# Matmuls chained in program order from the first token block on, with finer steps between blocks and attention and a two-step weight preparation

## The chip, the core and the metric

The kernel runs on one core of a Trainium2 chip. The metric is the device time of one execution in microseconds (us); lower is better. The engines are TensorE (PE; PEld for its weight loads), VectorE (DVE), ScalarE (ACT), GpSimd (POOL) and SyncE (SP), which here only issues the DMAs. Each engine works through its own queue in the order in which the program was built; semaphores tie the queues together.

## What is computed

```python
# attention, q, k, v: (4, 8, 576, 64); rows see columns of their own and earlier blocks of 64
scores = q @ k.T / 8, masked
attn = softmax(scores)
x = (attn @ v) as (2304 tokens, 512)
# layer 1:  d_model 512, d_ff 1536
x = ((x @ w_a) * (x @ w_b)) @ w_out
# layer 2:
xn = x / sqrt(mean(x * x) + 1e-6) * rms_g
g = xn @ w_gate
out = (g * sigmoid(g) * (xn @ w_val)) @ w_out
```

All is float32. Matmuls take numbers of fewer bits, so most operands are split into a high and a low part, and one product becomes three matmuls (high by high, high by low, low by high).

## The kernel before

**Blocks.** The 2304 tokens are cut into five blocks (512, then four of 448 columns), which pass through layer 1 (b0 to b4) and then layer 2 (b5 to b9). In a block, `moe` runs over 12 slices of d_ff, `fc`. A slice takes 24 matmuls, called A here (L444 to L446, `mm<-xh,ab`). After every three slices follow 36 matmuls with the second weights, called O (L471 to L473, `mm<-hh,o`). A block thus has 288 A and 144 O. Between A and O stand the product `g` on DVE (L456) and its parts `hh` (ACT) and `hl` (POOL, or DVE for the last slice of three).

**Attention.** The 32 heads (8 per batch of 576 tokens) come from the generator `attention`. For head m it issues scores S (L289, L290: tile i of up to 128 rows has 128, 256, 384, 512 and, in two halves of 288, 576 columns), transposes T of head m-1 (L336, in groups of 4, 5, 5 and 1), and values V of head m-2 (L375). A score tile goes to DVE for its row maximum (L293, L295, L298), to ACT for the exponential (L301) and to POOL for the division by the row sum (L315). A transposed group is copied as `ph` by ACT (L353) and `pl` by DVE (L354). Scores have two PSUM banks, so tile i+2 waits until tile i has been read.

**How they are mixed.** Layer 1's block b0 needs batch 0, b1 the next, and so on. `main` and `att` are streams: after each step of `main` the loop lets `att` go on while it is behind a share (`PACE`) of the matmul time spent in `main`. If heads are missing when the last O of a block are near, `before_last` issues them all. It then calls `split_of`, which makes `xh` and `xl` of the next block; they have one buffer, so the block before must have read them.

**Weights.** `prepare` takes one of 72 pieces of weights through `decode` (ACT L131 and L132, DVE L133 and L134, POOL L135) and then `split` (high part ACT, low part DVE or POOL by turns). Layer 1's pieces are used at once and written to DRAM for later blocks; 9 are made before b0 and 27 in b0. Layer 2's 36 pieces are made in b1 to b4.

**What sets the order.** The framework's scheduler takes the instructions from the program and decides each engine's order at build time, by priority and by a model of when operands are ready. `behind` adds an order edge without a semaphore. Before the change no such edge concerns PE: the scheduler may move A, O, S, T and V past each other.

Of the kernel before, what the change touches and what calls it, by code (L numbers as in the profile page):

```python
# [16 lines left out]
P = 128  # L17
# [29 lines left out]
def tile_attention_moe_moe(  # L47
# [30 lines left out]
    wab = ctx.enter_context(tc.tile_pool(name="wab", bufs=3))  # L78
# [39 lines left out]

    def decode(st):
# [8 lines left out]
        dst = stage.tile([P, 4 * P], F32, tag="x", name="x", bufs=2)  # L128
# [18 lines left out]
    staged, prepared, wtiles = {}, [0], {}  # L147
# [9 lines left out]
    def prepare():  # L157

        i = prepared[0]
        if i >= len(w_pieces):  # L160
            return
        stage_loads(i + 3)
        layer, kind, f, y = w_pieces[i]
# [11 lines left out]
        x = decode(staged.pop(i))  # L175
        prepared[0] += 1
# [34 lines left out]
    def attention(pools, x_of, done):  # L211
# [62 lines left out]
        def score(m, i):  # L274
# [12 lines left out]
            for a, z in halves:  # L287
                ps = ps_s()
                pe.matmul(ps[:, 0:z - a], qh[:, o:nk], kk[:, a:z], start=True, stop=False)  # L289
                pe.matmul(ps[:, 0:z - a], ql[:, o:nk], kk[:, a:z], start=False, stop=True)  # L290
                pss.append(ps)
# [26 lines left out]
        def p_transposes(m):  # L318
            pt[m] = []
            at = [0, 0]  # L320
            for part, pieces in GROUPS:
# [12 lines left out]
                for o, j, i, perm in first + rest:  # L334
                    a = min(j * P, S - P)
                    pe.transpose(ps[:, o:o + P], pp[m, i][:, a:a + P], perm)  # L336
                    cost += P / 1.2
# [21 lines left out]
        def values(m):  # L359
# [5 lines left out]
            for a, e in ((0, R), (R, S)):  # L365
# [22 lines left out]
            del vv[m], pt[m]  # L388
            done[b] = done.get(b, 0) + 1
            return cost  # L390
# [6 lines left out]
        for m in range(NH + 2):  # L397
            if m >= 2:
                yield values(m - 2)
# [28 lines left out]
    def moe(layer, pools, xh, xl, n, ps_mm, acc, finish, before_fc, before_last):  # L428
        hp, tp = pools
        h = {}  # L430
        for t in range(NTH):
            fcs = range(t * TF, (t + 1) * TF)
            for fc in fcs:
# [5 lines left out]
                for wi in range(2):  # L439
                    ps = ps_mm()  # L440
                    wh, wl = w[:, 2 * wi, :], w[:, 2 * wi + 1, :]
                    for c in range(KC):
                        a, z = c * P, (c + 1) * P
                        pe.matmul(ps[:, 0:n], wh[:, a:z], xh[:, c, 0:n], start=(c == 0), stop=False)  # L444
                        pe.matmul(ps[:, 0:n], wh[:, a:z], xl[:, c, 0:n], start=False, stop=False)  # L445
                        pe.matmul(ps[:, 0:n], wl[:, a:z], xh[:, c, 0:n], start=False, stop=(c == KC - 1))  # L446
# [11 lines left out]
                    yield KC * mm3(n)  # L458
# [3 lines left out]
            for dm0 in range(0, KC, 2):  # L462

                banks = {dm: ps_mm() for dm in (dm0, dm0 + 1)}
                for ys in (range(TF - 1), range(TF - 1, TF)):
                    for dm, ps in banks.items():
                        for y in ys:
# [84 lines left out]
    n = 0  # L552
# [8 lines left out]
    def normed(t0, n):  # L561
# [15 lines left out]
        pe.matmul(ps[:, 0:n], rms["ones"], sh, start=True, stop=False)  # L577
        pe.matmul(ps[:, 0:n], rms["ones"], sl, start=False, stop=True)
# [15 lines left out]
    nxt = split_of(0, BLOCKS[0])  # L594
    for at, (layer, t0, n_tok) in enumerate(blocks):
# [14 lines left out]
        def before_fc(fc, at=at, layer=layer, following=following, norm=norm, got=got):  # L610
            if at == 0:
                if fc > 0:
                    for _ in range(TF):
                        if prepared[0] < len(w_pieces) // 2:
                            prepare()
            else:
# [4 lines left out]
                if layer == 0:  # L621
                    n = sum(BACKGROUND[:at]) + BACKGROUND[at] * (fc + 1) // FC
                    while prepared[0] < len(w_pieces) // 2 + n:
                        prepare()
# [95 lines left out]
```

## Time and profile before

| what | us |
|---|---|
| median of 3 runs (1185.93 to 1188.22) | 1187.19 |
| the profiled execution, its own time | 1193.02 |
| its span, first to last instruction | 1191.2 |
| PE busy in the span | 1132.8 |
| DVE, ACT, POOL busy | 710.1, 529.5, 489.1 |

The span is what the trace explains; times below are counted from its start. A busy PE is not PE at its full rate, because the records of matmuls overlap; how far apart matmuls start says more.

### The profile page before, as it was taken

The page shows a single profiled execution, that of the slowest core. Times are in us where ns is not written, and L with a number is a line of the kernel's source. Part 1 is how long each engine was busy: PE and PEld are TensorE (multiplying, and loading weights), DVE is VectorE, ACT ScalarE, POOL GpSimd, SP SyncE. Part 2 cuts the span into 40 slices and gives each one's busy share as a digit, 9 for nine tenths or more (in the row PEclk, how much of TensorE's full clock was granted, in tenths as well). Part 3 has the DMA queues.
Part 4 walks back from the last instruction along what each step waited for, and adds up shares of the span by engine and source line. Part 5 has one row for each costly group of instructions (what it writes and reads, how often), then busy time and mean ns, then how long its engine had stood idle before and what let it go on. Part 6 is the DMA issues. An engine that isn't in the chain of part 4 may idle for free.

```text
span 1191.2 us, 16081 instructions
## 1 busy us (share of the span) xinstructions
PE 1132.8 (95%) x5578; PEld 992.0 (83%) x5578; DVE 710.1 (60%) x1411; ACT 529.5 (44%) x1174; POOL 489.1 (41%) x474
## 2 busy tenths in 40 slices
PE   7888888989999889998999999999999999999998
PEld 5566667769989779898899998888999999999997
DVE  7869799997777787778945523323624534433222
ACT  7758776765655666556533312312312312211211
POOL 6748767776636565546535202112012112112110
PEclk9898988999999889999899999999999999999999
DMA  5436575879777667658898956655765765765760
GB/s 177 147 113 217 192 260 173 311 251 335 261 239 240 229 234 234 230 203 309 310 412 323 341 198 246 224 195 191 279 228 198 280 221 204 256 214 209 255 227 35
DMA packets 65905, 279.98 MB, mean 235 GB/s; under 512 B 12064, under 2 KB 22304, under 8 KB 45344
## 3 DMA queue, kind: packets, MB, share of 16 engines
q1 hardware_dynamic: 65824, 278.95, 66.3%
q8 instruction: 44, 0.72, 0.2%
q14 instruction: 37, 0.30, 0.1%
HBM read 231.74 MB, written 47.19 MB: 234 GB/s over the span
## 4 chain that ended last, share of the span: by engine, by line
PE 67%; DVE 9%; ACT 4%; DMA 3%; POOL 2%; issue 2%; DVEq 0%; POOLq 0%; ACTq 0%
PE mm L445 14%; PE mm L446 14%; PE mm L444 14%; PE mm L471 7%; PE mm L472 7%; PE mm L473 7%; PE t L336 2%; PE t L375 2%; POOL x L135 1%; DVE kk L254 1%; DVE x L133 1%; PE s L289 1%; DVE st L134 1%; PE s L290 1%; DVE pl L354 1%
## 5 line engine op out<-in xcount | busy, mean ns | idle before, releaser
L444 PE MATMUL mm<-xh,ab 128*128 128x448 f32 (+1 forms) x960 | 360.2, 377 | 6.1 <-DVE xf L387 2.1
L446 PE MATMUL mm<-xh,ab 128*128 128x448 f32 (+1 forms) x960 | 358.7, 374 | 0.3 <-POOL ab L107 0.2
L445 PE MATMUL mm<-xl,ab 128*128 128x448 f32 (+1 forms) x960 | 358.3, 373 | 0.0
L107 POOL TENSOR_TENSOR hl<-g,hh 128x448 fp32r<-128x448 f32 (+1 forms) x80 | 99.4, 1243 | 425.1 <-ACT hh L97 424.5
L444 PEld LDWEIGHTS mm<-xh,ab 128*128 128x128 f32 x960 | 181.5, 189 | 26.3 <-ACT ab L97 2.9
L446 PEld LDWEIGHTS mm<-xh,ab 128*128 128x128 f32 x960 | 181.6, 189 | 19.9 <-POOL ab L107 0.4
L445 PEld LDWEIGHTS mm<-xl,ab 128*128 128x128 f32 x960 | 181.9, 190 | 18.3
L471 PE MATMUL mm<-hh,o 128*128 128x448 f32 (+1 forms) x480 | 182.3, 381 | 5.0 <-ACT hh L97 3.5
L472 PE MATMUL mm<-hh,o 128*128 128x448 f32 (+1 forms) x480 | 179.4, 374 | 0.0
L473 PE MATMUL mm<-hl,o 128*128 128x448 f32 (+1 forms) x480 | 169.1, 374 | 0.9 <-POOL hl L107 0.9
L97 ACT ACTIVATE hh<-g 128x448 fp32r<-128x448 f32 (+1 forms) x120 | 70.5, 588 | 204.2 <-DVE g L456 203.7
L315 POOL TENSOR_SCALAR p<-p,st 128x128 f32<-128x128 f32 (+4 forms) x160 | 106.5, 677 | 106.4 <-DVE st L312 63.9
L456 DVE SCALAR_TENSOR_TENSOR g<-mm,asb 128x448 f32<-128x448 f32 (+1 forms) x120 | 76.1, 635 | 117.5 <-PE mm L446 116.6
L135 POOL TENSOR_TENSOR x<-x,st 128x512 uint32<-128x512 uint32 x72 | 104.9, 1461 | 70.3 <-DVE st L134 27.1
L453 DVE SCALAR_TENSOR_TENSOR asb<-mm,asb 128x448 f32<-128x448 f32 (+1 forms) x60 | 38.2, 636 | 144.7 <-ACT asb L452 144.7
L301 ACT ACTIVATE p<-s,st 128x128 f32<-128x128 f32 (+2 forms) x171 | 88.5, 520 | 69.3 <-DVE st L295 40.7
L481 DVE SCALAR_TENSOR_TENSOR acc<-mm,acc 128x448 f32<-128x448 f32 (+1 forms) x120 | 69.9, 627 | 70.6 <-PE mm L473 70.5
L471 PEld LDWEIGHTS mm<-hh,o 128*128 128x128 f32 x480 | 90.9, 190 | 18.2 <-ACT hh L97 5.3
L473 PEld LDWEIGHTS mm<-hl,o 128*128 128x128 f32 x480 | 90.3, 189 | 11.7 <-POOL hl L107 1.7
L452 ACT ACTIVATE asb<-mm 128x448 f32<-128x448 f32 (+1 forms) x60 | 33.4, 556 | 148.1 <-PE mm L446 148.1
L472 PEld LDWEIGHTS mm<-hh,o 128*128 128x128 f32 x480 | 91.3, 190 | 9.1
L336 PE MATMUL t<-ident,p 128*128 128x128 f32 x416 | 73.2, 295 | 3.1 <-POOL p L315 2.9
(99 smaller groups left out, 1645.2 us busy)
## 6 DMA issues: line engine op xcount, KB each, us to landing
ab<-wab SPq DMA_DIRECT2D x108, 1024.0 KB, 6.0
o<-wo SPq DMA_DIRECT2D x36, 1536.0 KB, 6.9
st<-in_w_ab_dram SPq DMA_DIRECT2D x48, 512.0 KB, 4.5
wab<-ab SPq DMA_DIRECT2D x12, 1024.0 KB, 4.5
st<-in_w_o_dram SPq DMA_DIRECT2D x24, 512.0 KB, 4.9
wab<-bg SPq DMA_DIRECT2D x24, 512.0 KB, 7.0
qr<-in_q_dram SPq DMA_DIRECT2D x64, 144.0 KB, 3.8
wo<-o SPq DMA_DIRECT2D x4, 1536.0 KB, 6.2
```

What stands on the lines that cost most here:

```text
L107: eng_lo.tensor_tensor(lo, src, hi.bitcast(F32), ALU.subtract)
L135: pool.tensor_tensor(x, x, lo, ALU.add)
L301: act.activation(pi[:, a:z], pss[x][:, 0:z - a], AF.Exp, bias=s[:, i:i + 1], scale=1.0, accum_out=s[:, 5 + i + x:6 + i + x],)
L315: pool.tensor_scalar(pi, pi, s[:, 5 + y:6 + y], 1.0, ALU.mult, ALU.mult)
L336: pe.transpose(ps[:, o:o + P], pp[m, i][:, a:a + P], perm)
L444: pe.matmul(ps[:, 0:n], wh[:, a:z], xh[:, c, 0:n], start=(c == 0), stop=False)
L445: pe.matmul(ps[:, 0:n], wh[:, a:z], xl[:, c, 0:n], start=False, stop=False)
L446: pe.matmul(ps[:, 0:n], wl[:, a:z], xh[:, c, 0:n], start=False, stop=(c == KC - 1))
L456: dve.scalar_tensor_tensor(g, ps[:, 0:n], UNSCALE, asb, ALU.mult, ALU.mult)
L471: pe.matmul(ps[:, 0:n], wh, hh, start=(y == 0), stop=False)
L472: pe.matmul(ps[:, 0:n], wl, hh, start=False, stop=False)
L473: pe.matmul(ps[:, 0:n], wh, hl, start=False, stop=(y == TF - 1))
```

## The change

Every matmul and transpose now goes through a helper that, once b0 begins, puts it behind the one that the program issued before it: the scheduler can no longer reorder PE. The generators yield after every three A or three O and after each half of the values, so that the program itself mixes them. `prepare` decodes one piece and splits the piece of the call before; `x` has three buffers and `wab` four. Pieces are paced by the time spent in the block instead of by slice.

```diff
-    wab = ctx.enter_context(tc.tile_pool(name="wab", bufs=3))
+    wab = ctx.enter_context(tc.tile_pool(name="wab", bufs=4))
...
+    def in_order(ins):
+        if fixed[0] and "pe" in gate:
+            behind(ins, "pe")
+        gate["pe"] = ins
+    def matmul(*args, **kw):
+        in_order(pe.matmul(*args, **kw))
+    def transpose(*args):
+        in_order(pe.transpose(*args))
...
-        dst = stage.tile([P, 4 * P], F32, tag="x", name="x", bufs=2)
+        dst = stage.tile([P, 4 * P], F32, tag="x", name="x", bufs=3)
...
     def prepare():
         i = prepared[0]
+        if decoded:
+            split_piece(*decoded.pop())
         if i >= len(w_pieces):
             return
         stage_loads(i + 3)
+        decoded.append((i, decode(staged.pop(i))))
+        prepared[0] += 1
+        if prepared[0] in (len(w_pieces) // 2, len(w_pieces)):
+            split_piece(*decoded.pop())
...
                 for y, (src, j, q0) in enumerate(seq):
-                    pe.matmul(
+                    matmul(
...
-            del vv[m], pt[m]
-            done[b] = done.get(b, 0) + 1
-            return cost
+                if a > 0:
+                    del vv[m], pt[m]
+                    done[b] = done.get(b, 0) + 1
+                yield cost
+                cost = 0.0
...
-                        pe.matmul(ps[:, 0:n], wl[:, a:z], xh[:, c, 0:n], start=False, stop=(c == KC - 1))
+                        matmul(ps[:, 0:n], wl[:, a:z], xh[:, c, 0:n], start=False, stop=(c == KC - 1))
+                        if c < KC - 1:
+                            yield mm3(n)
...
-                    if ys[-1] == TF - 1:
-                        continue
-                    yield 2 * (TF - 1) * mm3(n)
+                            if y < TF - 1:
+                                yield mm3(n)
...
     nxt = split_of(0, BLOCKS[0])
+    fixed[0] = True
...
+        total = (2 * FC * KC + FC * KC) * mm3(n_tok)
+        first = prepared[0]
+        more = (BACKGROUND[at] if at else len(w_pieces) // 2 - first) if layer == 0 else 0
         while main.step():
+            while prepared[0] - first < min(more, int(more * main.spent / total / 0.85 + 0.9)):
+                prepare()
```

In the changed program PE's instructions carry the helper's lines, L128 for matmuls and L131 for transposes; DVE's L313 to L374 are the L293 to L354 of before.

**The end of b1 on PE.** `mm<-hh,o` are the last O of b1, `mm<-xh,ab` the first A of b2, `vv` the values of the second last head that b2 needs. Before:

```order
L375 MATMUL t<-ph_4412,vv 128x64
L471 MATMUL mm<-hh,o 128x448
L472 MATMUL mm<-hh,o 128x448
L473 MATMUL mm<-hl,o 128x448
L471 MATMUL mm<-hh,o 128x448
L472 MATMUL mm<-hh,o 128x448
L473 MATMUL mm<-hl,o 128x448
L471 MATMUL mm<-hh,o 128x448
L472 MATMUL mm<-hh,o 128x448
L473 MATMUL mm<-hl,o 128x448
L444 MATMUL mm<-xh,ab 128x448
L445 MATMUL mm<-xl,ab 128x448
```

After, where the values are those of the last head that b2 needs:

```order
L128 MATMUL t<-ph_4648,vv 128x64
L128 MATMUL t<-pl_4649,vv 128x64
L128 MATMUL mm<-xh,ab 128x448
L128 MATMUL mm<-xl,ab 128x448
L128 MATMUL mm<-xh,ab 128x448 x2
L128 MATMUL mm<-xl,ab 128x448
L128 MATMUL mm<-xh,ab 128x448 x2
L128 MATMUL mm<-xl,ab 128x448
L128 MATMUL mm<-xh,ab 128x448
L128 MATMUL mm<-hh,o 128x448 x2
L128 MATMUL mm<-hl,o 128x448
```

Before, a score, transposes and the values of one more head stand among the first A of b2. Now all heads of b2 stand ahead of 9 A and all 36 last O of b1.

**A head's last transpose and its values on PE, in b1.** `t<-swap` at the head of the rows is the last transpose group of a head, the one of 64 columns. Before:

```order
L336 MATMUL t<-swap,p_3212 128x128
L289 MATMUL s<-kk,qh 128x384
L290 MATMUL s<-kk,ql 128x384
L473 MATMUL mm<-hl,o 128x448 x2
L289 MATMUL s<-kk,qh 128x512
L290 MATMUL s<-kk,ql 128x512
L473 MATMUL mm<-hl,o 128x448
L375 MATMUL t<-ph_3334,vv 128x64
L375 MATMUL t<-pl_3335,vv 128x64
L471 MATMUL mm<-hh,o 128x448
L472 MATMUL mm<-hh,o 128x448
L473 MATMUL mm<-hl,o 128x448
```

After:

```order
L131 MATMUL t<-swap,p_3415 128x128
L128 MATMUL t<-ph_3525,vv 128x64
L128 MATMUL t<-pl_3526,vv 128x64
L128 MATMUL mm<-xh,ab 128x448
L128 MATMUL mm<-xl,ab 128x448
L128 MATMUL mm<-xh,ab 128x448
L128 MATMUL t<-ph_3525,vv 128x512
L128 MATMUL t<-pl_3526,vv 128x512
L128 MATMUL t<-ph_3525,vv 128x448
L128 MATMUL t<-pl_3526,vv 128x448
L128 MATMUL t<-ph_3606,vv 128x320
L128 MATMUL t<-pl_3607,vv 128x320
```

Before, nine more matmuls of the block follow the rows shown, and then the ten values. Now only three A stand between; two values of 192 columns follow, and then the pair that needs the last transpose.

**DVE ahead of the copy `pl` of that last transpose, in b1.** Before:

```order
L293 MEMSET s 64x64
L295 TENSOR_REDUCE st<-s 128x1
L354 TENSOR_TENSOR pl_3177<-t,ph_3176 128x512
L293 MEMSET s 64x64
L134 SCALAR_TENSOR_TENSOR st<-st 128x512
L354 TENSOR_TENSOR pl_3177<-t,ph_3176 128x64
```

After:

```order
L318 TENSOR_REDUCE st<-s 128x1
L99 CAST qh<-qr 128x576
L318 TENSOR_REDUCE st<-s 128x1
L274 SCALAR_TENSOR_TENSOR kk<-kr,kk 64x576
L374 TENSOR_TENSOR pl_3186<-t,ph_3185 128x64
```

Now the two maxima of the 288-column scores and the key product `kk` of the next head stand ahead of the copy.

## Rows read from the trace of the kernel before

**Rows 1.** Windows: stretch, then busy us per engine; clock, DMA share, GB/s.

```profile
0.00:101.80 101.80, 81.47 (x367) 55.59 (x368) 79.59 (x227) 73.34 (x189) 66.36 (x79) 0.90 0.48 151
101.80:270.80 169.00, 151.27 (x707) 120.40 (x705) 153.66 (x301) 118.40 (x268) 128.70 (x114) 0.93 0.69 239
270.80:395.80 125.00, 124.14 (x699) 114.71 (x698) 93.38 (x228) 73.54 (x186) 72.66 (x81) 1.00 0.75 261
395.80:545.30 149.50, 139.99 (x753) 125.21 (x752) 113.22 (x266) 87.72 (x221) 85.55 (x97) 0.95 0.68 232
425.00:545.30 120.30, 118.50 (x662) 107.40 (x662) 92.70 (x212) 70.94 (x178) 68.25 (x76) 1.00 0.70 237
545.30:647.90 102.60, 97.01 (x460) 88.07 (x459) 67.73 (x92) 50.07 (x92) 49.26 (x39) 0.95 0.90 343
737.20:835.60 98.40, 98.40 (x436) 81.44 (x435) 33.38 (x49) 25.35 (x40) 14.66 (x11) 1.00 0.60 215
835.60:1186.40 350.80, 350.80 (x1732) 325.06 (x1731) 133.65 (x203) 77.51 (x137) 50.11 (x41) 1.00 0.61 218
```

**Rows 2.** Timeline of PE around the starts of b2 and b3.

```profile
405.18 0.33 PE L289 MATMUL s<-kk,qh 128*128 128x128 f32 x1 [2.65 <-ACT p L301]
...
418.58 1.07 PE L444 MATMUL mm<-xh,ab 128*128 128x448 f32 x3 [1.98 <-DVE xh L99]
...
421.67 0.69 PE L289 MATMUL s<-kk,qh 128*128 128x384 f32 x1 [1.17 <-ACT p L301]
...
557.57 0.47 PE L444 MATMUL mm<-xh,ab 128*128 128x448 f32 x1 [2.08 <-DVE xf L387]
```

**Rows 3.** Groups by line, PE, 270.8 to 395.8: counts of S, T, V.

```profile
L336 PE MATMUL t<-ident,p 128*128 128x128 f32 x89 | 14.4, 275 | 0.0
L290 PE MATMUL s<-kk,ql 128*128 128x288 f32 (+4 forms) x40 | 12.5, 313 | 0.0
...
L375 PE MATMUL t<-pl,vv 128*128 128x64 f32 (+4 forms) x41 | 11.9, 315 | 0.0
```

**Rows 4.** Groups by line, DVE, 101.8 to 270.8: last column the idle time before.

```profile
L107 DVE TENSOR_TENSOR o<-x,o 128x512 fp32r<-128x512 f32 x11 | 10.5, 957 | 1.2 <-ACT o L97 1.0
...
L107 DVE TENSOR_TENSOR ab<-x,ab 128x512 fp32r<-128x512 f32 x9 | 7.9, 880 | 2.6 <-ACT ab L97 2.6
```

**Rows 5.** Timeline of PE: transposes at 353, then values of one head.

```profile
352.74 0.82 PE L336 MATMUL t<-ident,p 128*128 128x128 f32 x6
353.40 0.27 PE L336 MATMUL t<-swap,p 128*128 128x128 f32 x1
...
301.45 0.39 PE L375 MATMUL t<-ph,vv 128*128 128x512 f32 x1
...
302.80 0.21 PE L375 MATMUL t<-ph,vv 128*128 128x64 f32 x1
```

**Rows 6.** Timeline: DVE's copies `pl` (the first after 353.40), and a late transpose's.

```profile
354.94 0.79 DVE L354 TENSOR_TENSOR pl<-t,ph 128x512 fp32r<-128x512 f32 x2
...
388.30 0.27 PE L336 MATMUL t<-swap,p 128*128 128x128 f32 x1
...
392.92 0.21 DVE L354 TENSOR_TENSOR pl<-t,ph 128x64 fp32r<-128x64 f32 x1
```

**Rows 7.** Timeline: scores of 512 columns on PE and their exponentials on ACT, twice.

```profile
279.29 0.39 PE L290 MATMUL s<-kk,ql 128*128 128x512 f32 x1
...
283.45 0.67 ACT L301 ACTIVATE p<-s,st 128x512 f32<-128x512 f32 x1
...
337.67 0.39 PE L290 MATMUL s<-kk,ql 128*128 128x512 f32 x1
...
339.43 0.69 ACT L301 ACTIVATE p<-s,st 128x512 f32<-128x512 f32 x1 [1.14 <-DVE st L295]
```

**Rows 8.** Groups by line and shape, DVE, 270.8 to 395.8: mean ns after busy us.

```profile
L254 DVE SCALAR_TENSOR_TENSOR kk<-kr,kk 64x576 fp32r<-64x576 f32 x7 | 10.8, 1544 | 0.6 <-ACT kk L252 0.4
...
L298 DVE TENSOR_REDUCE st<-s 128x1 f32<-128x288 f32 x12 | 5.4, 448 | 1.4 <-PE t L375 1.1 <-PE s L290 0.3
...
L354 DVE TENSOR_TENSOR pl<-t,ph 128x64 fp32r<-128x64 f32 x7 | 1.5, 208 | 0.0
```

**Rows 9.** Timeline of DVE: low part of the sum of squares, layer 2.

```profile
747.78 1.22 DVE L107 TENSOR_TENSOR sl<-sq,sh 128x448 fp32r<-128x448 f32 x1 [0.65 <-ACT sh L97]
```

More of the change, by code (lines that the diff above doesn't have):

```diff
@@ L288, in score @@
                 ps = ps_s()
-                pe.matmul(ps[:, 0:z - a], qh[:, o:nk], kk[:, a:z], start=True, stop=False)
-                pe.matmul(ps[:, 0:z - a], ql[:, o:nk], kk[:, a:z], start=False, stop=True)
+                matmul(ps[:, 0:z - a], qh[:, o:nk], kk[:, a:z], start=True, stop=False)
+                matmul(ps[:, 0:z - a], ql[:, o:nk], kk[:, a:z], start=False, stop=True)
                 pss.append(ps)
@@ L335, in p_transposes @@
                     a = min(j * P, S - P)
-                    pe.transpose(ps[:, o:o + P], pp[m, i][:, a:a + P], perm)
+                    transpose(ps[:, o:o + P], pp[m, i][:, a:a + P], perm)
                     cost += P / 1.2
@@ L398, in attention @@
             if m >= 2:
-                yield values(m - 2)
+                yield from values(m - 2)
             sc = list(tiles) if m < NH else []
@@ L470, in moe @@
                             wh, wl = wo[:, 0, a:a + P], wo[:, 1, a:a + P]
-                            pe.matmul(ps[:, 0:n], wh, hh, start=(y == 0), stop=False)
-                            pe.matmul(ps[:, 0:n], wl, hh, start=False, stop=False)
-                            pe.matmul(ps[:, 0:n], wh, hl, start=False, stop=(y == TF - 1))
-                    if ys[-1] == TF - 1:
-                        continue
-                    yield 2 * (TF - 1) * mm3(n)
+                            matmul(ps[:, 0:n], wh, hh, start=(y == 0), stop=False)
+                            matmul(ps[:, 0:n], wl, hh, start=False, stop=False)
+                            matmul(ps[:, 0:n], wh, hl, start=False, stop=(y == TF - 1))
+                            if y < TF - 1:
+                                yield mm3(n)
                 for dm, ps in banks.items():
@@ L576, in normed @@
         ps = ps_r.tile([P, 512], F32, tag="r", name="r")
-        pe.matmul(ps[:, 0:n], rms["ones"], sh, start=True, stop=False)
-        pe.matmul(ps[:, 0:n], rms["ones"], sl, start=False, stop=True)
+        matmul(ps[:, 0:n], rms["ones"], sh, start=True, stop=False)
+        matmul(ps[:, 0:n], rms["ones"], sl, start=False, stop=True)
         dve.tensor_scalar(sq, ps[:, 0:n], 1.0 / DM, 1e-6, ALU.mult, ALU.add)
@@ L610, in before_fc @@
         def before_fc(fc, at=at, layer=layer, following=following, norm=norm, got=got):
[L611 to L616, printed above, removed]
+            if at > 0:
                 if fc % TF == 0:
@@ L620, in before_fc @@
                     fetch_ab(layer, fc + 2)
[L621 to L624, printed above, removed]
             if following and fc + 2 >= FC:
```

11 lines of the change are left out of this document (5 added, 6 removed).

## The prediction, made before the changed kernel ran

> **What bounds the kernel now.** I first read the windows by stage [rows 1]. From 647.9 us on (the last block of layer 1 and all of layer 2) PE never rests: the four blocks from 835.6 to 1186.4 take 350.8 us, 87.7 us for 432 matmuls of 448 columns, with the granted clock at 1.00; the 512-column block before them takes 98.4. There an order can win nothing. So whatever the change brings lies before 647.9. In b0 (its A run in earnest from 101.8 us; only 27 of them stand earlier in the order) DVE is busy 153.7 of 169.0 us: DVE sets the pace there, PE has slack. In b1 PE is busy 124.1 of 125.0: PE is the bound. In b2 (149.5 us) and b3 (102.6) neither is full; PE has 9.5 and 5.6 us of idle and a clock of 0.95.
>
> The timeline of PE then shows where b2 and b3 lose [rows 2]. At 405.18 a score waits 2.65 us for its bank, at 418.58 the first slice of b2 waits for `xh` of the fourth channel group, at 557.57 the first slice of b3 waits the same way. These are block starts: the last heads that the new block needs are still under way, and little else is left that PE could do. The rest of b2 is clean: 425.0 to 545.3 has 1.8 us of idle and a clock of 1.00 [rows 1].
>
> **The change part by part.** I make the sum against the profiled span, 1191.2 us (that execution's own time was 1193.02; the median of the runs is 1187.19), and carry the difference over to the median.
>
> *Block starts.* What does attention cost PE? b1 of before, which is PE-bound, took 125.0 us, 87.7 of them for its A and O; 37.3 remain for attention. The counts [rows 3] give 40 of 6 score pairs a head, 89 of 13 transposes by the identity, 41 of 6 low value matmuls: 6.8 heads, thus 5.5 us a head and 43.9 for eight. In the changed order b1 holds 8 heads, b2 8 heads without the scores of one (about a third of a head, 1.8 us, an estimate), b3 none, and all heads that a block needs stand 45 matmuls or more before its first A, about 9 us, in which `xf`, `xh` and `xl` are made. PE alone then needs 87.7 + 43.9 = 131.6 us for b1, 129.8 for b2 and 87.7 for b3, 349.1 together, where before 125.0 + 149.5 + 102.6 = 377.1 went by. Gain 28.0, if no new wait appears.
>
> *New waits.* The price of a fixed order is that a matmul that waits holds every A and O behind it. Two places are tight. First, a head's last transpose and the values that use it: in between stand now three A (0.61 us) and ten values, of which two are short and eight take 1.35 [rows 5], so about 2.05 us from the end of the transpose's record. In before the copies behind the transposes of 353.40 and 388.30 (records that end at 353.67 and 388.57) were done at 355.73 and 393.13, 2.06 and 4.56 us later [rows 5, 6]. Second, the 512-column scores and the second half of the next tile, which takes their bank: nine A (1.83), five transposes (0.11 each [rows 5]) and the other half (0.3, an estimate) stand between, about 2.55 us. In before the exponential was done 2.06 us after one such score and 4.44 after another [rows 7]. So a head may pay nothing, or 2.5 + 1.9 = 4.4 us. To choose, I put the mean durations [rows 8] into DVE's changed order. From the first half of the last score tile to the copy stand two maxima (0.45 each), `qh` (about 0.6), `kk` (1.54) and the copy (0.21), 3.25 us, while PE has 3.8 us of matmuls until it needs the copy. That fits when nothing more is queued. In the order of b1 and b2 six of 16 heads have one piece of 0.6 to 0.8 us more ahead of the copy (a `g`, another `pl`), two have several; I price the six at 0.4 and the two at 4 together, 6.4 us, and as much again for the score banks: 12 us, 0.75 a head, nearer the short end.
>
> *b0.* Its start moves little: PE does the 27 early A after 101.8 instead, and needs 98.4 + 43.9 = 142.3 us for the whole block against 153.7 us of work on DVE. So DVE stays the bound, and PE can lose 2.9 us a head before it matters. The two-step `prepare` takes one thing off DVE: the low parts `ab` and `o` no longer queue right behind the high parts from ACT. DVE stood idle 2.6 and 1.2 us for them [rows 4]; I take these 3.8 us, 165.2 instead of 169.0. The ends: 153.7 with DVE never idle, and 142.3 + 8 x 4.4 = 177.5 if every head of b0 pays both long waits.
>
> *At nothing.* The third `x` and the fourth `wab` buffer only let decodes and fetches start earlier; a slice's 24 A take 4.9 us, and none of PE's waits in [rows 2] is for a fetch. The two matmuls of each norm in layer 2 are now tied to a place 120 A and 36 O into a block, 31.7 us. Before, `sl` was ready at 749.0 [rows 9], and in ACT's and DVE's changed orders these sums stand in the block before. If that cover went, PE would stop in five blocks. The finer steps and pacing add no instruction. 0 to 101.8 and 647.9 to 1191.2 stay as they are.
>
> *Sum.* 101.8 + 165.2 + 349.1 + 12 + 543.3 = 1171.4, 19.8 less than the span. The median becomes 1167.
>
> *The clock.* In the windows [rows 1] b2 has 6% idle, part of it in waits of two us, and a clock of 0.95; its rest, with 1.8 us of short waits in 120, has 1.00. My 12 us in 261 are short waits, so I take nothing. The Trainium skill (TensorE: Matmul & The Clock Gate, Part 1) says that the clock is throttled by default and that activity releases it, which speaks against a queue that stops for every late operand. By that rule, with b2's 0.95 over both blocks, the sum would be 13 us more, 1180. The trace agrees only for long waits.
>
> **The rivals.**
>
> *No price.* The queues follow the new order, nobody waits, and DVE in b0 is nearly full: 101.8 + 153.7 + 349.1 + 543.3 = 1147.9, a median of 1144; to 1156 with some waits. For it: the short chains [rows 6, 7] just fit. Against: over the whole of b0 DVE came to 91%.
>
> *The waits eat it all.* Each head stops PE twice, since nothing may pass. Place: values behind the copy, and scores behind their bank, in b1 and b2. It decides from (28.0 + 3.8) / 16 = 2.0 us a head on; at 2.6 the sum is 101.8 + 165.2 + 349.1 + 41.6 + 543.3 = 1201.0 and the median 1197. For it: the late copies and exponentials [rows 6, 7], and `kk` ahead of the copy in the changed order. Against: these chains were long where nobody waited for them, and a PE that stands lets DVE, 75% busy in b1, catch up.
>
> *The clock drops with the short waits*, 1180, as worked out above.
>
> *It does not reach the block starts.* If ACT and DVE bring the last heads of b2 and b3 no sooner than before, the 45 matmuls pass, PE stops as before [rows 2], and the gain shrinks to b0's few us less the waits: no change, 1187. Against: from 395.8 to 425.0 DVE was busy 113.2 - 92.7 = 20.5 of 29.2 us [rows 1], so it was not full.
>
> **How the numbers follow.** Forecast (1156 to 1180) 0.60, no price 0.14, waits eat it 0.15, clock 0.06, block starts not reached 0.05. 0.2% of the time, 2.4 us, is about what a measurement can tell. Faster: 0.60 + 0.14 + 0.04 of the clock's case = 0.78; same 0.05 + 0.02 = 0.07; slower 0.15. With 0.05 below and 0.13 above, the range is 1147 to 1191.
>
> **What would show it.** Right: no wait for `xh` or a score's bank at the starts of b2 and b3; b3 at about 88 us; b1 longer than before, near 137; b2 near 136; many waits under 1 us, of values on `pl` and scores on ACT's `p`. b0 should end near 267. Wrong: b1 and b2 over 145, or b0's end beyond 280 because DVE now waits for a PE that stands; a clock under 0.98 in b1; an idle PE ahead of the norm's matmuls in layer 2.

## The result and the profile after

The changed kernel takes 1204.84 us (median of 4 runs, 1201.10 to 1206.74), the kernel before 1186.56 (4 runs, 1185.30 to 1188.22). The ratio is 1.0149 with a 95% interval of 1.0119 to 1.018: slower by 1.5%, where 1167 was forecast. The profiled execution has a span of 1205.0 us (its own time is 1206.74); the sum had 1171.4. Medians here and below leave out one slow execution, the profiled one of g2_all_distances, which took 3837.57 us.

Windows by stage of the changed kernel, the columns as in [rows 1]; the stretches are b0 from 101.8 us on, b1, b2, b3, and b6 to b9:

```profile
101.80:272.40 170.60, 145.91 (x694) 119.78 (x694) 149.56 (x298) 116.27 (x265) 120.36 (x112) 0.94 0.70 243
272.40:420.10 147.70, 136.27 (x745) 122.39 (x744) 119.12 (x264) 85.25 (x215) 86.86 (x95) 0.98 0.72 240
420.10:567.00 146.90, 134.26 (x734) 121.04 (x734) 113.45 (x246) 85.17 (x209) 81.67 (x88) 0.98 0.67 230
567.00:655.30 88.30, 88.06 (x433) 80.98 (x432) 43.77 (x62) 38.72 (x70) 39.23 (x30) 1.00 0.96 365
...
844.50:1201.00 356.50, 353.97 (x1735) 324.77 (x1733) 133.60 (x205) 82.01 (x140) 49.68 (x41) 1.00 0.60 212
```

Against the sum, b0 ends 5.4 us late, b1 and b2 take 294.6 us instead of 131.6 + 129.8 + 12 = 273.4 (21.2 more), b3 0.6 more, and the rest, 655.3 to 1205.0, 549.7 instead of 543.3 (6.4 more): 33.6 in all, which is the whole difference. The block starts came as forecast: the first A of b2 (420.13) and of b3 (566.99) wait for nothing, and b3 is full.

The waits of PE in b1 and b2 of the changed kernel (what waits and for whom; us in total, times, longest):

```profile
PE s L128 <- ACT p L321: 6.7, 7, 2.1
PE mm L128 <- DVE st L319: 5.1, 2, 2.9
PE mm L128 <- DVE hl L107: 3.8, 3, 1.6
PE t L128 <- DVE st L319: 3.4, 2, 2.9
PE t L128 <- DVE pl L374: 1.9, 4, 1.2
PE mm L128 <- ACT hh L97: 1.6, 2, 1.1
PE mm L128 <- DVE acc L504: 1.4, 1, 1.4
```

`s` are the scores behind their bank and `t` the values behind the copy `pl`, the two places that were priced. `mm` on `hl`, `hh` or DVE's `st L319` are O, which wait for the parts of the last slice of three: a third place, which was not priced and, taken as one, is the costliest (5.1 + 3.8 + 1.6 = 10.5 of the 23.9 us; the scores have 6.7, the values 5.3; the last 1.4 are a bank that DVE's sum `acc` had not yet read). (`st L319` is the tiny maximum queued right behind `hl` or `pl`; DVE's semaphore shows that one.) Two of these waits, first PE, then DVE, in each pair of fences:

```profile
301.26 0.74 PE L128 MATMUL mm<-hl,o 128*128 128x448 f32 x1 [2.27 <-DVE st L319]
...
484.96 0.27 PE L131 MATMUL t<-swap,p 128*128 128x128 f32 x1
...
490.38 0.30 PE L128 MATMUL t<-pl,vv 128*128 128x64 f32 x1 [2.91 <-DVE st L319]
```

```profile
298.26 1.81 DVE L107 TENSOR_TENSOR bg<-x,bg 128x512 fp32r<-128x512 f32 x1
299.99 0.68 DVE L148 SCALAR_TENSOR_TENSOR st<-st 128x512 uint32<-128x512 uint32 x1
300.59 0.61 DVE L107 TENSOR_TENSOR hl<-g,hh 128x448 fp32r<-128x448 f32 x1
...
486.81 1.78 DVE L274 SCALAR_TENSOR_TENSOR kk<-kr,kk 64x576 fp32r<-64x576 f32 x1
488.62 1.57 DVE L107 TENSOR_TENSOR hl<-g,hh 128x448 fp32r<-128x448 f32 x1
490.11 0.21 DVE L374 TENSOR_TENSOR pl<-t,ph 128x64 fp32r<-128x64 f32 x1
```

In the first case two instructions of layer 2's weight preparation (2.33 us from 298.26 to the start of `hl`) stand ahead of `hl`, in the second a key product and `hl` stand ahead of the copy `pl`. DVE never rests in either stretch (no line has an idle time): what PE waits for is the queue in front of the instruction, not the instruction. The preparation's share of that queue, from the groups by line and shape of DVE, 272 to 567 us:

```profile
L148 DVE SCALAR_TENSOR_TENSOR st<-st 128x512 uint32<-128x512 uint32 x24 | 25.6, 1065 | 1.2 <-ACT st L145 1.0
L147 DVE TENSOR_SCALAR x<-a 128x512 uint32<-128x512 uint32 x21 | 17.6, 839 | 0.2
...
L107 DVE TENSOR_TENSOR bg<-x,bg 128x512 fp32r<-128x512 f32 x7 | 7.5, 1071 | 0.0
```

That is 50.7 of DVE's 232.6 busy us in b1 and b2.

In layer 2, where no attention is left, b6 to b9 take 356.5 us instead of 350.8 [rows 1]. By the first A of each block, b6 to b8 take 89.7 us each (before: 88.0, 88.0 and 87.6) and b9, in which no norm for a next block is made, 87.4 to the end of the window (before: 87.3). The timeline of b6 (PE, then DVE): the reciprocal of the norm delays `g` (883.41), and the first O on the last slice waits for `hh`.

```profile
884.69 0.66 PE L128 MATMUL mm<-hh,o 128*128 128x448 f32 x2 [0.71 <-ACT hh L97]
```

```profile
879.53 2.95 DVE L605 RECIPROCAL y<-y 128x448 f32<-128x448 f32 x1 [2.07 <-ACT y L604]
...
883.41 0.62 DVE L480 SCALAR_TENSOR_TENSOR g<-mm,asb 128x448 f32<-128x448 f32 x1
```

### The profile page after: what moved, and what is told of

The parts are those of the page before. It is cut to its first block, busy times and chain, and to the rows that moved or that the text cites. A ratio compares the mean times of both kernels' runs of the same rounds, so it can differ in the third digit from the quotient of the medians.

```text
span 1205.0 us, 16045 instructions
## 1 busy us (share of the span) xinstructions
PE 1127.0 (94%) x5578; PEld 987.5 (82%) x5578; DVE 717.7 (60%) x1411; ACT 533.4 (44%) x1176; POOL 482.4 (40%) x474
## 4 chain that ended last, share of the span: by engine, by line
PE 63%; DVE 18%; ACT 6%; issue 5%; DMA 4%; POOL 3%; SPq 1%; DVEq 0%; POOLq 0%; ACTq 0%
PE mm L128 57%; DMA st<-in_w_ab_dram 2%; DVE st L148 2%; DVE x L147 2%; PE t L131 2%; PE s L128 2%; PE t L128 2%; ACT p L321 1%; DVE st L315 1%; DVE pl L374 1%; DMA st<-in_w_o_dram 1%; DVE hl L107 1%; DVE g L480 1%; DVE y L605 1%; DVE kk L274 1%
## 5 line engine op out<-in xcount | busy, mean ns | idle before, releaser
L128 PE MATMUL mm<-xh,ab 128*128 128x448 f32 (+1 forms) x1920 | 600.7, 377 | 0.0
L128 PEld LDWEIGHTS mm<-xh,ab 128*128 128x128 f32 x1920 | 363.8, 189 | 36.8
L128 PE MATMUL mm<-xl,ab 128*128 128x448 f32 (+1 forms) x960 | 357.7, 373 | 0.0
L128 PE MATMUL mm<-hh,o 128*128 128x448 f32 (+1 forms) x960 | 284.9, 378 | 6.6 <-ACT hh L97 5.0
L128 PEld LDWEIGHTS mm<-hh,o 128*128 128x128 f32 x960 | 179.0, 191 | 26.9 <-ACT hh L97 8.1
L128 PE MATMUL mm<-hl,o 128*128 128x448 f32 (+1 forms) x480 | 182.6, 380 | 14.4 <-DVE hl L107 9.2
L128 PEld LDWEIGHTS mm<-xl,ab 128*128 128x128 f32 x960 | 182.3, 190 | 16.3
L128 PEld LDWEIGHTS mm<-hl,o 128*128 128x128 f32 x480 | 91.7, 191 | 31.5 <-DVE hl L107 22.0
L504 DVE SCALAR_TENSOR_TENSOR acc<-mm,acc 128x448 f32<-128x448 f32 (+1 forms) x120 | 74.2, 633 | 51.8 <-PE mm L128 49.9
L128 PE MATMUL s<-kk,qh 128*128 128x128 f32 (+2 forms) x171 | 60.3, 357 | 23.9 <-ACT p L321 23.6
L148 DVE SCALAR_TENSOR_TENSOR st<-st 128x512 uint32<-128x512 uint32 x72 | 71.4, 994 | 8.8 <-ACT st L145 8.4
L374 DVE TENSOR_TENSOR pl<-t,ph 128x512 fp32r<-128x512 f32 x96 | 54.6, 569 | 25.0 <-ACT ph L373 22.9
L131 PE MATMUL t<-ident,p 128*128 128x128 f32 x416 | 66.5, 285 | 1.8 <-POOL p L335 1.7
L146 ACT ACTIVATE a<-st 128x512 f32<-128x512 f32 x72 | 48.1, 668 | 42.1 <-DMA st<-in_w_ab_dram 16.8
```

The source lines that it names most:

```text
L128: in_order(pe.matmul(*args, **kw))
L131: in_order(pe.transpose(*args))
L146: act.activation(a, hi.bitcast(F32), AF.Copy, scale=2.0 ** -111)
L148: dve.scalar_tensor_tensor(lo, hi, 0x80000000, lo, ALU.bitwise_and, ALU.bitwise_or)
L374: dve.tensor_tensor(both[1], ps[:, 0:n], both[0].bitcast(F32), ALU.subtract)
L504: dve.scalar_tensor_tensor(acc[:, dm, 0:n], ps[:, 0:n], UNSCALE, acc[:, dm, 0:n], ALU.mult, ALU.add)
```

## The experiments

### Which part of the change costs

The tie is the edge that puts each matmul behind the one issued before it. e1_no_chain takes it away and keeps all else:

```diff
-    fixed[0] = True
```

> Order theory: the chain of matmuls is what costs. Without it the scheduler keeps 5 to 6 us of PE work between a slice's last A and the O on its hh, 6 us behind the 512-column scores and 7 us behind a head's last transpose, so b1 to b3 and layer 2 go back to what they were: about 1187 us (1181 to 1193). Rival, the two-step weight preparation and its pacing cost: nothing of that is undone, so about 1200 to 1205.

e2_chain_alone ties the order of the kernel before, with its coarse steps and its old preparation:

```diff
-                pe.matmul(ps[:, 0:z - a], qh[:, o:nk], kk[:, a:z], start=True, stop=False)
...
+                matmul(ps[:, 0:z - a], qh[:, o:nk], kk[:, a:z], start=True, stop=False)
...
+    fixed[0] = True
```

> Order theory: the chain over the old, coarse steps leaves still less work between a score and the next use of its bank (0.7 us in places) and 1.6 us between the last transpose and its values, so it waits more than the change does: 1210 to 1230 us. Rival, weight preparation: the old preparation is back, so about 1187 us.

e3_chain_to_b2 unties PE once attention has ended:

```diff
             attn.close()
+            fixed[0] = False
```

> The chain ends with b2. Order theory: the 6.4 us that the profile after shows beyond 655 us come from O standing 2.4 us behind the last A of its slice instead of 5.3; they go, b0 to b2 stay: 1198 us (1194 to 1201). Rival, that something else in the change slows layer 2 (four wab buffers, the fetches): no difference, about 1205.

e4_old_prepare has the tie and the fine steps, with the preparation, its pacing and its buffers of before:

```diff
-        decoded.append((i, decode(staged.pop(i))))
+        x = decode(staged.pop(i))
...
+        split_piece(i, x)
```

> The chain and the fine steps with the weight preparation, pacing and buffers of before. Order theory: within 5 us of the change, 1200 to 1210. Rival, weight preparation costs: most of the 18 us come back, 1187 to 1192.

| kernel | median us | ratio to before, 95% |
|---|---|---|
| e1_no_chain | 1191.34 | 1.0056 (1.0032 to 1.0081) |
| e2_chain_alone | 1223.21 | 1.0299 (1.0257 to 1.034) |
| e3_chain_to_b2 | 1196.67 | 1.0098 (1.0073 to 1.0123) |
| e4_old_prepare | 1212.20 | 1.0225 (1.0197 to 1.0253) |

These four were timed beside a kernel before of 1185.02, the changed kernel beside one of 1186.56; so differences to the changed kernel are given twice, by the medians and by the ratios. The tie costs 13.5 or 11 us and is the larger part of the loss, not all of it: without it the kernel is still 0.6% slower than before, clear of noise. 8 or 6 us return when the tie ends after b2; by the first A of each block b6 to b9 then take what they took before (88.0, 88.0, 87.6, 87.7). Under the tie the fine steps save 11 us (1223 to 1212), nearly all of it in b1 and b2, which take 301.5 us in e2_chain_alone and 291.9 in e4_old_prepare, and the two-step preparation 7 or 9, not in b1 and b2 (294.6 with it). Without the tie the stops at the block starts are back: PE's waits of e1_no_chain from 395 to 660 us begin with

```profile
PE t L131 <- POOL p L335: 6.3, 2, 4.9
PE mm L128 <- DVE xh L99: 5.1, 1, 5.1
```

With them b1, b2 and b3 of e1_no_chain take 376.7 us together, as before (377.1).

### Are producer and consumer too close in PE's order?

My first theory after the result was that each wait is a distance: in b1 and b2 of the tied order PE has only 2.4 to 4.9 us of matmuls between the last A of a slice and the O on its `hh`, and 2.2 to 2.8 us between a head's last transpose and its values (4.1 to 5.9 and 5.5 to 7.6 in the order before; the matmuls that stand between, each at the usual time from start to start of its kind, 0.2 us for 448 columns). Three kernels widen one distance each, a fourth moves the norm, and a fifth widens three.

f1_three_banks:

```diff
-            for dm0 in range(0, KC, 2):
-                banks = {dm: ps_mm() for dm in (dm0, dm0 + 1)}
+            for dms in ((0, 1, 2), (3,)):
+                banks = {dm: ps_mm() for dm in dms}
...
```

> The changed kernel with the second weights' matmuls grouped by output banks as three and one instead of two and two, so that more matmuls stand between the last A of a slice and the first O on its hh and hl: 3.7 and 4.1 us of matmuls instead of 2.4 and 2.8 in layer 2, 6.1 to 6.7 in most slices of b1 and b2. Theory 1 (the O that stand too close behind hh and hl cost about 13.5 us in b1 and b2 and nearly all of the 6 us in layer 2): the waits on hh and hl go, layer 2's blocks return to 88.0, b1 and b2 lose 8 to 13 us together, 1188 to 1195 us in all. Theory 2 (these waits only take turns with others: the head's own chains set the pace of b1 and b2, and the norm that of layer 2): b1 and b2 stay within 3 us, 1202 to 1206.

f2_last_transpose:

```diff
+                if alive and len(sc) == 1:
+                    c = next(ct, None)
...
+                        yield c
                 if sc:
                     yield score(m, sc.pop(0))
```

> The changed kernel with the last group of a head's transposes issued before the last score tile instead of behind it: 3.4 to 4.6 us of matmuls instead of 2.2 between the last transpose and the values that read its copy. Theory 1 (the values wait since they stand too close): the values' waits, about 6 us in b1 and b2, and a part of the bank waits go, b0 ends 2 to 5 us sooner, 1193 to 1199 us. Theory 2 (the copy is late because DVE is late with all of a head's work, wherever it stands in PE's order): the copy now waits for the softmax, the transposes wait instead, 1202 to 1208.

f3_split_tile4, in which `score` yields between its halves:

```diff
+                if z < nk:
+                    yield 2 * max(107.0, (z - a) / 2.4)
```

> The changed kernel with a slice's A between the two halves of each score tile, so that 3.3 us instead of 2.7 stand between the 512 columns and the next tile's second half, which takes their bank. Theory 1 (each score that waits for its bank is short of cover by 0.3 to 0.9 us): about half of the 8.5 us of bank waits in b1 and b2 go, b0 ends 2 to 4 us sooner, 1198 to 1202. Theory 2 (bank waits follow ACT's lateness with the whole head): nothing, 1203 to 1207.

f5_norm_slice4:

```diff
-            if fc in (3, 5, 7):
+            if fc in (3, 4, 7):
```

> The changed kernel with the last norm matmul and what hangs on it (square root, reciprocal, r) one slice earlier, in fc 4 instead of fc 5, which is no longer the slice right before a group of O. Theory 1 (in layer 2 the square root with its two table loads and the reciprocal of 2.95 us delay hh and hl of the slice whose O come 2.4 us behind): b5 to b8 lose 1 to 1.7 us each, 1199 to 1201. Theory 2 (the O wait because they stand too close, whether a norm is there or not): layer 2 stays, 1203 to 1206. b1 and b2 are unchanged by either.

g2_all_distances is f1, f2 and f3 together:

> The changed kernel with three distances widened at once: banks of the second weights as three and one, the last transposes before the last score tile, A between the halves of a score tile. Theory 1 (each wait of b1 and b2 is a producer that stands too close in PE's order): with all of them widened nothing is left to wait for, b1 and b2 take 133 to 138 us each, 1172 to 1184 us in all. Theory 2 (the order of PE only decides which matmul waits; b1 and b2 take 147 us because DVE's and ACT's queues, which carry eight heads and ten pieces of layer 2's weight preparation in each of these blocks, deliver a head every 18 us): b1 and b2 stay at 143 us or more, and only layer 2's 6 us come back, 1193 to 1202.

| kernel | median us | ratio to before, 95% | b1 + b2 us |
|---|---|---|---|
| changed | 1204.84 | 1.0149 (1.0119 to 1.018) | 294.6 |
| f1_three_banks | 1198.29 | 1.0106 (1.0075 to 1.0137) | 294.7 |
| f2_last_transpose | 1210.47 | 1.0224 (1.0181 to 1.0267) | 298.5 |
| f3_split_tile4 | 1211.27 | 1.022 (1.0189 to 1.0251) | 295.8 |
| f5_norm_slice4 | 1213.35 | 1.0231 (1.0189 to 1.0273) | 293.7 |
| g2_all_distances | 1199.79 | 1.0115 (1.0082 to 1.0147) | no trace at its usual time |

(The three executions of g2_all_distances took 1197.66 to 1201.06.)

For b1 and b2 the theory fell: whichever of the three distances is widened, they take as long as in the changed kernel or longer, and all three together are no faster than f1_three_banks alone, where the theory asked for 1172 to 1184. The waits only change places. The waits of PE in these blocks, first of f1_three_banks, where those on `hh` and `hl` are nearly gone and the values wait 8.7 + 3.6 = 12.3 us instead of 5.3:

```profile
PE t L128 <- DVE pl L374: 8.7, 4, 3.5
PE s L128 <- ACT p L321: 6.8, 7, 1.9
...
PE t L128 <- DVE st L319: 3.6, 4, 1.1
PE mm L128 <- DVE hl L107: 1.7, 1, 1.7
```

Then of f2_last_transpose, where the values wait no more and the O wait 13.4 us on `hl`:

```profile
PE mm L128 <- DVE hl L107: 13.4, 7, 3.6
PE s L128 <- ACT p L321: 10.2, 11, 2.1
```

It does not follow that distance never counts in b1 and b2: the coarse steps of e2_chain_alone made them 9.6 us longer than the fine ones.

For layer 2 the theory holds: f1_three_banks has 3.7 us instead of 2.4 ahead of the O, and b6 to b9 are back at 352.0 us without a wait (its window from 841.1):

```profile
841.10:1193.10 352.00, 352.00 (x1735) 325.26 (x1733) 133.65 (x204) 81.90 (x140) 49.78 (x41) 1.00 0.59 216
```

f5_norm_slice4 made layer 2 worse (b6 to b9 take 364.8 us), against what I expected. The reciprocal did move a slice ahead, but what follows it now stands in DVE's queue in front of the last slice's `g`:

```profile
882.86 2.46 DVE L612 SCALAR_TENSOR_TENSOR xf<-xf,rms_g,y 128x448 f32<-128x448 f32 x4
885.24 0.61 DVE L480 SCALAR_TENSOR_TENSOR g<-mm,asb 128x448 f32<-128x448 f32 x1
```

The first O behind it waits 1.81 us, where the changed kernel waits 0.71.

### Is DVE's queue too full?

The second theory: a head comes as fast as DVE and ACT can deliver it, and ten pieces of preparation in each block stand among the heads' instructions. h1_prep_later makes none in b1 and b2, and 18 pieces in b3 and b4 each:

```diff
-BACKGROUND = (0, 10, 10, 10, 6)
+BACKGROUND = (0, 0, 0, 18, 18)
```

> The changed kernel with the 20 pieces of layer 2's weights that b1 and b2 prepare moved to b3 and b4 (18 pieces each there, where DVE is about half busy and there is no attention); PE's order and all distances stay. Theory 2 (DVE's and ACT's queues are late with the heads, since ten pieces a block stand among them): b1 and b2 fall by 6 to 12 us each, to 135 to 141, b3 and b4 stay within 2 us of 88.3 and 89.8, 1182 to 1194 us in all. Theory 1 (producer and consumer stand too close in PE's order, whatever else DVE does): b1 and b2 stay at 144 or more, 1200 to 1206. A third: b3 and b4 pay for the pieces what b1 and b2 save.

h2_prep_later_banks adds the edit of f1_three_banks:

> The same move of the preparation together with the second weights' banks as three and one. Layer 2 gets back 6 us as it did with the banks alone; by theory 2 b1 and b2 take 135 to 141 us each and the whole is 1175 to 1188 us, below the kernel before if it is under 1182. By theory 1 the banks help b1 and b2 only once other distances are widened too: 1193 to 1199.

h3_before_prep_later is the same move in the kernel before:

> The kernel before with the same move of the preparation to b3 and b4, its order left to the scheduler. If the load of DVE and ACT in b1 and b2 also sets when the last heads of b2 and b3 come, the stops at the block starts shrink and b2 and b3 lose 5 to 12 us together: 1173 to 1181. If these stops are a matter of the order alone (DVE was not full there), no change: 1183 to 1190.

| kernel | median us | ratio to before, 95% |
|---|---|---|
| h1_prep_later | 1190.88 | 1.0038 (1.0023 to 1.0054) |
| h2_prep_later_banks | 1193.65 | 1.0061 (1.0039 to 1.0083) |
| h3_before_prep_later | 1177.09 | 0.9928 (0.9897 to 0.9958) |

The windows of b1, b2, b4 and b5 of h1_prep_later:

```profile
267.40:400.50 133.10, 131.25 (x745) 120.51 (x744) 92.96 (x241) 69.69 (x186) 60.83 (x78) 1.00 0.56 187
400.50:535.60 135.10, 131.18 (x733) 119.81 (x732) 92.56 (x227) 71.57 (x183) 59.79 (x73) 0.99 0.53 183
...
623.50:717.60 94.10, 90.93 (x435) 82.57 (x434) 45.84 (x67) 39.38 (x68) 36.48 (x27) 0.98 0.91 328
717.60:826.90 109.30, 103.02 (x435) 83.24 (x434) 56.83 (x83) 42.74 (x72) 43.28 (x31) 0.97 0.81 302
```

With PE's order and every distance unchanged, b1 and b2 fall by 26.4 us to 268.2, and their waits to

```profile
PE mm L128 <- DVE hl L107: 4.1, 3, 1.9
PE t L128 <- DVE pl L374: 1.3, 2, 0.7
```

b4 and b5 give 14.2 of it back: the moved pieces load the DMA queues (a share of 0.91 in b4 instead of 0.72), and the last of them is split at 800 us, inside b5, where DVE has 56.8 us of work instead of 39.5. Of PE's 6.3 us of idle time in b5, 1.1 are a wait for weights, 2.9 for `xh` and 2.3 for `hh` and `hl`. h2_prep_later_banks, of which I had expected 1175 to 1188 us, missed that: b1 and b2 take 268.1 us, but b5 119.0, and its longest wait is one for weights:

```profile
PE mm L128 <- DMA o<-wo: 8.1, 1, 8.1
```

A piece brings DVE time, ACT time, GpSimd time and transfers that ACT's decodes wait for. Two kernels put back one of the first two into h1_prep_later, on a scratch tile, in 20 units for the 20 pieces of b1 and b2. i1_dve_load:

```diff
+            while at in (1, 2) and extra < min(10, int(10 * main.spent / total / 0.85 + 0.9)):
+                extra += 1
+                scr = stage.tile([P, 4 * P], F32, tag="x", name="x", bufs=3)
+                dve.memset(scr, 1.0)
+                for _ in range(3):
+                    dve.tensor_tensor(scr, scr, scr, ALU.mult)
```

> The changed kernel with its preparation in b3 and b4 (18 pieces each), and in the places of the ten pieces of b1 and b2 only DVE work on a scratch tile, about 2.3 us each (one fill and three products of 512 columns), with no transfer, no ACT and no GpSimd work. Theory D (DVE's time is what the preparation takes from the heads): b1 and b2 return to 142 to 148 us each, 1202 to 1216 us in all. Theory A (ACT's decodes, which wait for transfers and hold ACT's queue, make the heads late): b1 and b2 stay at 133 to 138, 1189 to 1196.

i2_act_load, in the same loop:

```diff
+                pool.memset(scr, 1.0)
+                for _ in range(3):
+                    act.activation(scr, scr, AF.Copy)
```

> The same with ACT work on a scratch tile in those places instead, about 2 us each (three copies of 512 columns behind a fill by GpSimd), with no transfer and no DVE work. Theory D: b1 and b2 stay at 133 to 138 us, 1189 to 1196. A second form of theory A (ACT's own time): b1 and b2 rise to 142 to 148, 1202 to 1216. If neither this nor the DVE load brings the time back, the transfers that ACT's decodes wait for, or all together, are the cause.

i1_dve_load takes 1227.64 us (1.0335, 1.0293 to 1.0377), i2_act_load 1193.65 (1.0055, 1.0032 to 1.0079). The units wait for no transfer, so the scheduler put all of them between 246.2 and 325.2 us, at the end of b0 and in b1, not in b2 as I had assumed, and i1_dve_load lies above its range of 1202 to 1216. The windows of b0 and b1 of i1_dve_load, then those of i2_act_load:

```profile
83.70:287.00 203.30, 163.79 (x747) 133.08 (x747) 182.85 (x359) 125.38 (x286) 140.56 (x125) 0.89 0.64 221
287.00:439.10 152.10, 137.74 (x745) 125.04 (x745) 119.05 (x287) 71.13 (x188) 66.63 (x78) 0.96 0.49 163
```

```profile
83.40:273.40 190.00, 161.19 (x748) 132.28 (x748) 162.23 (x323) 136.09 (x309) 141.13 (x134) 0.90 0.67 237
273.40:408.40 135.00, 132.17 (x746) 120.50 (x744) 93.14 (x244) 88.72 (x226) 67.36 (x89) 1.00 0.55 184
```

The units' DVE work, by line and shape from 83.7 to 440 us, is 55.1 us:

```profile
L666 DVE TENSOR_TENSOR x<-x 128x512 f32<-128x512 f32 x60 | 45.4, 772 | 0.1
...
L664 DVE MEMSET x<- 128x512 f32 x20 | 9.7, 485 | 1.4 <-DVE kk L274 0.2 <-DVE xf L407 0.2
```

b0 to b2 take 490.7 us against 452.6 in h1_prep_later: 38.1 us of PE's time for 55.1 of DVE's. In i2_act_load, 60 copies of 0.63 us on ACT (37.6 us) cost 6.1, of which 5.6 in b0. So DVE's time alone is enough to bring such a loss, without transfers, and ACT's time alone is not. Two things stay open. GpSimd's part of the pieces (47.9 us less of its time in b1 and b2 of h1_prep_later) was not put back by itself, and the scratch units stood close together, where the pieces are spread, so the size of the loss is not theirs. And DVE's load is not all that counts in a tied order: with the coarse steps, b1 and b2 took their 301.5 us with DVE busy for only 213.3, where the fine ones took 291.9 with 227.9.

### Does the tie pay once DVE has room?

Both orders with eight of the pieces left in b1 and b2, the tied one with the banks of f1_three_banks (h4_prep_mid_banks), and the order before (h5_before_prep_mid):

```diff
-BACKGROUND = (0, 10, 10, 10, 6)
+BACKGROUND = (0, 4, 4, 14, 14)
```

> The changed kernel with the banks as three and one and only a part of the preparation moved: four pieces in b1 and b2 each, 14 in b3 and b4 each, so that b5's weights are ready in time. If the heads are late in proportion to DVE's load, b1 and b2 lie 40% of the way from 133 and 135 to 148 and 146, near 139 us, b5 returns to 98.4 to 102, 1177 to 1184 us in all; if they are late only when DVE is nearly full, b1 and b2 stay at 133 to 136, 1170 to 1176.

> The kernel before with the same partial move. Moving all of it gave 1177 with b5 2.5 us long; if b1 and b2 are insensitive to four pieces each, 1174 to 1177; if each piece costs its share of the 14 us that b2 got back, 1180 to 1184.

And both with four of them left and layer 2's low parts off DVE (j1_changed_best, with the banks, and j2_before_best):

```diff
-W_LO = ("dpd", "pdp")
+W_LO = ("dpd", "ppp")
...
+BACKGROUND = (0, 2, 2, 16, 16)
```

> The changed kernel with banks as three and one, two pieces of the preparation in b1 and b2 each and 16 in b3 and b4 each, and the low parts of layer 2's weights all on GpSimd, none on DVE. DVE has in b1 and b2 about 2 us a piece less than with ten pieces, 20 us less a block. If PE's loss there follows DVE's load, b1 and b2 take 134 to 137 us each; b5 takes 98.4 to 104 if its weights come in time: 1172 to 1179 us in all. If the transfers of 16 pieces in b4 are too many, b5 takes 105 to 110 and the whole is 1180 to 1188.

> The kernel before with the same two moves of the preparation. b2 takes 136 to 140 us, as with all or part of it moved, and b3 101: 1174 to 1179 us. If the fixed order is worth something once DVE has room, the changed kernel with these moves is more than 3 us below this one; if not, they are level.

| preparation | tied order, banks 3 + 1 | order before |
|---|---|---|
| as it was | 1198.29, 1.0106 (1.0075 to 1.0137) | 1184.52 on the same chip, 1 |
| 8 pieces | 1180.12, 0.9941 (0.9926 to 0.9957) | 1178.99, 0.9941 (0.9923 to 0.996) |
| 4 pieces, layer 2's low parts on GpSimd | 1183.26, 0.9969 (0.9951 to 0.9988) | 1177.38, 0.9921 (0.9898 to 0.9945) |
| none | 1193.65, 1.0061 (1.0039 to 1.0083) | 1177.09, 0.9928 (0.9897 to 0.9958) |

Three kernels with the order before and two with the tied one beat both kernels of this study. In no row is the tied order better. By blocks it is not so even. In b1, b2 and b3, where the tie was to win, the tied order takes 356.8 us with no piece, the order before 361.4; with eight pieces it is 364.0 against 366.1, with four 365.5 against 363.6. With no piece the tied kernel is 4.6 us ahead there and loses it from b4 on, by the late pieces and, without the banks of f1_three_banks, in layer 2. The kernel that unties PE after b2, as e3_chain_to_b2 does, and moves the preparation was not run.

b1 and b2 do not follow DVE's time in a straight line. With the banks of f1_three_banks throughout they take 268.1 us with no piece (DVE 188.7 busy), 276.5 with eight (208.9), 294.7 with twenty (237.8): 20.2 us of DVE's time cost 8.4 at first and 28.9 more cost 18.2. j1_changed_best, whose 1183.26 us lie above the 1172 to 1179 that I expected, has 199.0 of DVE's time and 276.2 us: less work there gave nothing against eight pieces. The windows of b1 and b2 of h4_prep_mid_banks, then of j1_changed_best, show where it went:

```profile
269.60:406.60 137.00, 131.47 (x746) 120.78 (x745) 102.67 (x248) 76.30 (x197) 70.07 (x84) 1.00 0.61 209
406.60:546.10 139.50, 131.58 (x734) 120.17 (x733) 106.22 (x233) 77.61 (x194) 70.22 (x80) 0.99 0.60 209
...
266.80:403.30 136.50, 132.83 (x745) 122.03 (x744) 98.87 (x243) 73.12 (x191) 65.77 (x81) 0.99 0.57 193
403.30:543.00 139.70, 132.83 (x734) 121.04 (x733) 100.17 (x228) 74.86 (x188) 66.33 (x78) 0.98 0.54 191
```

PE's idle time did fall, from 13.5 to 10.5 us, but its matmuls were busy 2.6 us longer, with the granted clock 0.01 lower in both blocks. Why the clock was lower is not shown.

## Why the prediction was wrong

**The step that failed is the price of the new waits.** It was 12 us in b1 and b2; it measured 294.6 - 131.6 - 129.8 = 33.2, or 2.1 a head. The two places that were priced, scores and values, cost 6.7 + 5.3 = 12.0, the very sum; that is luck, for in f1_three_banks the same two cost 19.1 and in f2_last_transpose 10.2. The other 21.2 were priced at nothing: 10.5 for the O behind `hh` and `hl`, the third place, 1.4 for a bank, and some 9 for matmuls that took longer. To price the third place would not have been enough, since the waits change places when a distance is widened. The larger fault is that I asked whether single chains fit a gap, with mean durations, and not how fast DVE gets through all that eight heads and ten pieces of preparation put into its queue. With the pieces gone, the same order took 268.2 us, 26.4 less. Mean durations hid a part: the value of 490.38 waited 2.91 us behind a key product of 1.78 and an `hl` of 1.57, one piece more ahead of the copy, which was priced at 0.4 with 1.54 for the product and 0.6 to 0.8 for the piece. A head came every 147.7 / 8 = 18.5 and 146.9 / 8 = 18.4 us; the forecast took 131.6 / 8 = 16.4 for granted, with the same ten pieces among them. In b1 of before it is 6.8 heads in 125.0 us [rows 1, 3], also one in 18.4, but that isn't shown to be DVE's pace: PE was full there, and with the pieces moved away (h3_before_prep_later) b1 of that order takes 124.5.

**The argument against the rival that came true** was that a standing PE lets DVE, 75% busy in b1, catch up. DVE was 79% busy in b1 and b2 of the changed kernel (232.6 of 294.6), and PE lost 2.1 us a head, 1.5 of them standing; at 69% (h1_prep_later) it waits almost never. The loss lay just above the rival's point of decision, 2.0 us a head. Its 2.6 a head was too much, and b0 and layer 2 added 11.8 us that it left out, so its median of 1197 came near the result in part by luck.

**PE's own need was nearly right.** Against 131.6 and 129.8 us for b1 and b2, PE is busy 131.25 and 131.18 us in h1_prep_later, where DVE has room. The block-start waits went, and b3 took 88.3 against 87.7.

**b0** was to end at 267.0 and ended at 272.4; in h1_prep_later, whose b0 is the same, it ended at 267.4. The 3.8 us of idle time that the two-step preparation was to take off DVE are gone but for 0.4 (0.1 ahead of `ab`, 0.3 ahead of `o`); what they brought can't be told from such a spread.

**Priced at nothing: everything from 647.9 on.** It cost 6.4 us. I had looked for a PE that waits ahead of the norm's matmuls; there is none. The tie fixed where those matmuls stand, so the norm's reciprocal of 2.95 us falls into the last slice ahead of a group of O, which stands 2.4 us behind in PE's order. In b6 to b9 f1_three_banks gives most of this back (352.0 of 356.5 us against 350.8), and e3_chain_to_b2 all of it.

**The clock** is 0.98 in b1 and b2, and 1.00 and 0.99 in h1_prep_later. The forecast took nothing for it, the rival 13 us by 0.95 (a sum of 1184; its 1180 is the median). The truth lies between: in b1 and b2 PE is idle 11.4 and 12.6 us, 24.0 of the 33.2; at most the other 9 can be matmuls at a lower clock. Between these two kernels the rule that I weighed, of the Trainium skill (TensorE: Matmul & The Clock Gate, Part 1), agrees with the trace in its direction. The sum of PE's idle time does not settle the clock, though: e2_chain_alone has 0.94 in b1 with 13.5 us of it and 1.00 in b2 with 14.8.

## What to carry to other kernels

Before fixing the order of one engine, work out the rate at which the engines that feed it can deliver in that stage, with all the background work in their queues, and compare it with the rate that the fixed order asks for; gaps between single producers and consumers come second, for a widened gap may only move the wait. When the waits keep their sum while they change places, take load off the common producer instead. Here a line that moves background work to stages where VectorE is half idle made the order before 0.6 to 0.8% faster; in the tied order with the banks of f1_three_banks it turned 1.1% slower than the kernel before into 0.3 to 0.6% faster where a part was left behind, which is level with the order before or behind it. Background work that is moved must still end in time and share the DMA queues, so move part of it. And tie only the stages that can win by it: the tie cost some 6 us in layer 2, where PE had not waited before.

## What was unexpected in the hardware

The same DVE instruction lasts from 0.6 to 1.8 us. Of the 32 `hl` of 448 columns in the trace of the changed kernel, the 17 beside which GpSimd has no record at all take 0.617 to 0.628 us; the ten beside which GpSimd works for nine tenths of their time or more take 0.81 to 1.81, the five between 0.60 to 1.57. The timeline of DVE at one of the ten and at one of the 17, then of GpSimd at the first (there is none at the second):

```profile
449.17 1.81 DVE L107 TENSOR_TENSOR hl<-g,hh 128x448 fp32r<-128x448 f32 x1
...
884.90 0.62 DVE L107 TENSOR_TENSOR hl<-g,hh 128x448 fp32r<-128x448 f32 x1
```

```profile
448.67 1.84 POOL L278 TENSOR_TENSOR ql<-qr,qh 128x576 fp32r<-128x576 f32 x1
```

The Trainium skill (GPSIMD Engine Reference, 1. Specifications) says that GpSimd shares its SBUF interfaces with VectorE, and that DVE instructions with two SBUF inputs contend for them; `hl` has two such inputs, and the trace agrees. So a mean duration from a stage where both engines work is no bound for a single instruction: the `kk` of 1544 ns in [rows 8] was 0.75 to 1.78 us here.
